# Reordering the side work of an attention and gated-unit kernel, and moving five kinds of loads

## The chip, the cores and the metric

The kernel runs on one core of a Trainium2 chip. The metric is the device time of one execution in microseconds; before the change it is 2025.47 us, the median of 3 runs (2024.54 to 2028.5). Times inside the kernel come from one profiled execution, which itself took 2024.75 us; its span from first to last instruction is 2022.6 us.

## The reference

Four batches of attention without a softmax, and then a gated linear unit over all 12032 rows. Shapes: u and v are 4 x 3008 x 256, z is 4 x 3008 x 64, w_gate and w_val are 256 x 1536 and w_out is 1536 x 256 (these three come in as 64-bit floats).

```python
scores = (1 / S) * z @ z.T            # per batch, S = 3008
attn = maximum(scores, 0) ** 2
x = u * (attn @ v)                    # 12032 rows of 256
gate = 1 / (1 + exp(-(x @ w_gate)))
out = (gate * (x @ w_val)) @ w_out
```

The scores of a batch are symmetric, so a block of them can be computed once and used turned for the mirrored block.

## The kernel before

**Two stages.** Attention fills the first 960 us of the span, the gated unit the rest. The change touches the first stage and the loads at its end. Every operand is split into a high and a low float32r part, so that three matmuls (or two, for the scores) make one product of full accuracy.

**Steps.** Attention is a list of 288 steps, 72 for each batch b: six chunks c of 512 queries (the last has 448), and for each chunk 12 pairs i of 128 keys, some computed and some mirrored from an earlier chunk. A step that is computed costs four score matmuls (L349, L350); ScalarE takes relu and square out of PSUM into the tile `r` (L357, L358) and rounds `r` to the high part `ah` (L373); VectorE subtracts to get the low part `al` (L378), and turns `r` for the mirrored blocks (L423, L427), which SP then stores to a DRAM tensor `shared` (L404, L409). A mirrored step loads its `r` back five steps ahead (L467) and goes straight to L373. Four steps of the first batch read blocks that were stored unturned (L464) and are turned late, on VectorE (L475). Then TensorE multiplies `ah` and `al` with the parts of v (L493, L495, L500). PSUM results of a chunk leave with one ScalarE copy (L515).

**Order within a step.** The order is written out by hand: the loop over g issues the scores of step g+2, the loads back of g+5, the stores of g, the turning of g+1, the late turning of g+2, then `run(before, g)`, then square, rounding and subtraction of step g+2, then `run(after, g)` and at last the matmuls of step g. Each engine works its own instructions in this order. `before` and `after` are tables of side work, filled ahead of the loop.

**Side work.** There are 18 jobs `Narrow`, which turn blocks of the 64-bit weights to float32 parts: each loads 512 KB of raw weights (L178), takes an absolute value on ScalarE one step later (L183), then bit operations on VectorE (L188 to L209), and stores the parts to DRAM (L233) for the second stage. Their first steps are 24 to 52, 84 to 126 and 156 to 198, seven steps apart; batch 3 (from step 216) has none. Other side work is the v of the next batch (load L293, high part L302, low part L308), its z (L258, L265, L268, L272), and at the end of attention the u rows (L551), their transposes (L559), the product x (L569), sums (L579) and parts (L583, L588) of the first group of the second stage, and the loads of its narrow weights (L603, L605).

All of these loads are issued by SP, one after the other. The raw areas are small rings: `raw_a` holds two v pairs and two pieces of z, `w_a` two raw weight blocks.

Of the kernel before, what the change touches and what calls it, by code (L numbers as in the profile page):

```python
# [26 lines left out]
def kernel(  # L27
# [16 lines left out]
    CH = 512  # L44
# [9 lines left out]
    def chunk(c):  # L54
        return min(CH, S - c * CH)
# [13 lines left out]
    v_a, z_a, zq_a, r_a, ah_a, al_a, al2_a, turned_a, raw_a, zt_a, keep_a, w_a, spare_a = map(area, sizes)  # L69
# [11 lines left out]
    def part(a, kb, cols, dt=F32):  # L81

        ap = a[:, int(kb * KB) : int(kb * KB) + cols]
        return ap if dt is F32 else ap.bitcast(dt)

    def f32(ap):
        return ap.bitcast(F32)
# [28 lines left out]
    def late(b, c):  # L116

        return (b, c) == (0, 0)

    def order(b, c):  # L120
        mirrored = [i for i in range(2 * c) if shared(b, i // 2, c)]
        own = [i for i in range(NPAIR) if i not in mirrored]
        last = []
        if halved(b, c):
            own.remove(2 * c + 1)
            last = [2 * c + 1]
        if not mirrored:
            return own + last
        own.sort(key=lambda i: (i // 2 > c, i // 2 < c and c < NCH - 1, i))
        m = len(own) + len(mirrored)  # L130
        places = [x * m // len(own) for x in range(len(own))]
        if (b, c) == (B - 1, NCH - 1):
            places = list(range(len(own)))
        line = [None] * m
        for x, i in zip(places, own):
            line[x] = i
        rest = iter(mirrored)
        return [next(rest) if i is None else i for i in line] + last

    steps = [(b, c, i) for b in range(B) for c in range(NCH) for i in order(b, c)]  # L140
    number = {s: g for g, s in enumerate(steps)}

    def back(s):
        return shared(s[0], s[2] // 2, s[1])
# [103 lines left out]
        return part(zq_a, 2 * ((b * NCH + p) % 2), CH, F32R)  # L248

    def load_z(b, p):  # L250
        t = part(w_a, 2 * p, CH) if b == 0 else part(raw_a, 4 + 2 * (p % 2), CH)
        t = t.rearrange("p (T d) -> p T d", d=32)
        n = chunk(p) // 32
        for g in range(4):
            d0 = 32 * (g % 2)
            src = z[b, p * CH : p * CH + 32 * n, d0 : d0 + 32].rearrange("(T p) d -> p T d", p=32)
            eng = nc.scalar if (b, p) == (0, 0) and g > 1 else nc.sync
            eng.dma_start(t[32 * g : 32 * g + 32, 0:n, :], src)  # L258
            if n < CH // 32:
                nc.sync.dma_start(t[32 * g : 32 * g + 32, n : n + 2, :], src[:, n - 2 : n, :])  # L260
        z_raw[b, p] = t.rearrange("p T d -> p (T d)")
# [8 lines left out]
    def z_low(b, p):  # L270
        hi, lo = z_place(b, p)
        nc.vector.tensor_tensor(lo, z_t[b, p], f32(hi), op=ALU.subtract)  # L272
# [13 lines left out]
        return (ap.rearrange("p (j d) -> p j d", j=2) for ap in (hi, lo))  # L286

    def load_v(b, i):
        t = part(turned_a, 2 * (i % 8), CH) if b == 0 else part(raw_a, 2 * (i % 2), CH)
        t = t.rearrange("p (j d) -> p j d", j=2)  # L290
        k0 = 256 * i
        if i < NPAIR - 1:
            nc.sync.dma_start(t, v[b, k0 : k0 + 256, :].rearrange("(p j) d -> p j d", j=2))  # L293
        else:
            nc.sync.dma_start(t[:, 0, :], v[b, k0 : k0 + P, :])
            for h in range(2):
                nc.sync.dma_start(t[64 * h : 64 * h + 64, 1, :], v[b, k0 + P : S, :])
        v_raw[b, i] = t
# [5 lines left out]
    def v_low(b, i):  # L304
        vh, vl = v_place(b, i)
        t = v_raw.pop((b, i))
        if i < NPAIR - 1:
            nc.vector.tensor_tensor(vl, t, f32(vh), op=ALU.subtract)  # L308
        else:
            nc.vector.tensor_tensor(vl[:, 0, :], t[:, 0, :], f32(vh[:, 0, :]), op=ALU.subtract)  # L310
            stacked = vh[64:128, 1, :]
            nc.vector.tensor_tensor(stacked, t[64:128, 1, :], f32(stacked), op=ALU.subtract)
# [6 lines left out]
    def r_of(s):  # L319
        return ring(r_a, 4, 5, s)  # L320

    def a_of(s):
        n = number[s] % 3
        al = part(al_a, 4 * n, 4 * KB, F32R) if n < 2 else part(al2_a, 0, 4 * KB, F32R)
        return ring(ah_a, 4, 3, s, F32R), al.rearrange("p (j q) -> p j q", j=2)
# [49 lines left out]
    def rest(s):  # L375
        n = chunk(s[1])
        r, (ah, al) = r_of(s), a_of(s)
        nc.vector.tensor_tensor(al[:, :, 0:n], r[:, :, 0:n], f32(ah[:, :, 0:n]), op=ALU.subtract)  # L378
# [74 lines left out]
    def as_stored(i):  # L453
        return part(keep_a, 4 * (i % 2), 2 * CH)
# [14 lines left out]
    def turn_late(s):  # L469
        b, c, i = s  # L470
        if back(s) and late(b, i // 2):
            src = as_stored(i).rearrange("p (B j a k) -> p k B j a", j=2, a=32, k=2)
            dst = r_of(s).rearrange("p k (B b j) -> p k B j b", b=32, j=2)
            for k in range(2):
                nc.vector.transpose(out=dst[:, k], in_=src[:, k])  # L475
# [230 lines left out]
    with tc.manual_schedule():  # L706
# [3 lines left out]
        before, after = {}, {}  # L710

        def at(when, g, f, *args):
            when.setdefault(g, []).append((f, args))

        def run(when, g):
            for f, args in when.get(g, ()):
                f(*args)

        per = NPAIR * NCH
        for b in range(1, B):  # L720
            g0 = (b - 1) * per
            for p in range(NCH):
                g = g0 + (3 * NPAIR + 4 * p if p < 3 else 4 * NPAIR + 4 * (p - 3) if p < 5 else 5 * NPAIR)
                if (b, p) == (1, 1):
                    g = 5 * NPAIR + 3
                at(after, g, load_z, b, p)
                at(before, g + 2, turn_z, b, p)
                at(before, g + 3, z_high, b, p)
                at(before, g + 3, z_low, b, p)
            line = [number[b - 1, NCH - 1, i] for i in range(NPAIR)]  # L730
            for i in range(1, NPAIR):
                line[i] = max(line[i], line[i - 1] + 1)
            for i in range(NPAIR):
                g = g0 + (2 * NPAIR + 4, 2 * NPAIR + 8, 3 * NPAIR + 2, 3 * NPAIR + 7)[i] if i < 4 else line[i - 4]
                at(after, g, load_v, b, i)
                at(before, g + 2, v_high, b, i)
                at(before, g + 2, v_low, b, i)
        for b in range(B):
# [3 lines left out]
        starts = [*range(24, 54, 7), *range(84, 127, 7), *range(156, 199, 7)][: 3 * NF]  # L742
        for n, g in enumerate(starts):
            job = Narrow(n)
            for x, name in enumerate(job.jobs):
                at(after if name in ("load", "store") else before, g + x, getattr(job, name))

        g = len(steps) - NPAIR  # L750
        for t in range(2):
            at(after, g, load_sums, 0, t)
        at(after, g, load_u, 0, 0)
        for i in (0, 1, 2):
            at(after, g, load_w, i)
        at(before, g + 2, turn_u, 0, 0)
        at(after, g + 2, load_u, 0, 1)
        at(before, g + 3, make_x, 0, 0)
        at(before, g + 4, turn_u, 0, 1)
        for i in (3, 4, 5, 7):  # L760
            at(after, g + 4, load_w, i)
        at(before, g + 5, make_x, 0, 1)
        for i in (T1, T3):
            at(before, g + 6, sum_x, 0, i)
# [56 lines left out]
        for g, (b, c, i) in enumerate(steps[:-2]):  # L821
            nxt = steps[g + 2]
            k = g % NPAIR
            early = g < NPAIR
            if g < 3:
                for _ in pe_pv(steps[g]):
                    pass
            pe_scores(nxt)
            if early:
                if k + 2 < NPAIR:  # L830
                    v_low(0, k + 2)
                if k + 5 < NPAIR:
                    load_v(0, k + 5)
                if k in (2, 3, 5):
                    z_low(0, {2: 3, 3: 4, 5: 5}[k])
                if k in (0, 2, 4):
                    turn_z(0, k // 2 + 3)
            if g + 5 < len(steps):
                load_back(steps[g + 5])
            if k == 1 and g > 1:  # L840
                keep(*steps[g - 2][:2], True)
            store_turned(steps[g])
            turn(steps[g + 1])
            turn_late(nxt)
            run(before, g)
            if not back(nxt):
                square(nxt)
            round_up(nxt)
            rest(nxt)
            if early and k + 3 < NPAIR:  # L850
                v_high(0, k + 3)
            if early and k in (1, 2, 4):
                z_high(0, {1: 3, 2: 4, 4: 5}[k])
            if k == 0 and g:
                keep(*steps[g - 1][:2], False)
            run(after, g)
            if g >= 3:
                for _ in pe_pv(steps[g]):
                    pass
# [51 lines left out]
        for J in range(last + 1):  # L911
# [29 lines left out]
            for c in (11, 22, 21, 12):  # L941
                f, t = c // 10 - 1, c % 10 - 1
# [47 lines left out]
```

## Time and profile before

| | |
|---|---|
| time, median of 3 runs | 2025.47 us |
| time of the profiled execution | 2024.75 us |
| span of the profiled execution | 2022.6 us |
| PE busy | 1951.4 us, 96% |
| DVE busy | 1381.6 us, 68% |
| ACT busy | 1115.9 us, 55% |
| mean granted TensorE clock | 0.987 |
| shares of the chain that ended last | PE 74%, DMA 7%, SPq 6%, ACT 5%, DVE 5%, issue 3% |

PE is TensorE, DVE VectorE, ACT ScalarE, POOL GpSimd; SPq is the queue in which SP issues transfers. The granted clock is a share of the full 2.4 GHz. The chain is followed back from the last instruction to whatever released each step.

### The profile page before, as it was taken

What the parts mean: (1) busy time and instruction counts of PE and PEld (TensorE: products, weight loads), DVE (VectorE), ACT (ScalarE), POOL (GpSimd) and SP (SyncE); (2) the same over time, 40 slices, a digit from 0 to 9 for tenths busy, and PEclk for the clock granted to TensorE, in tenths of its full rate; (3) what the DMA queues carried; (4) which work ended last, traced back from release to release, by engine and by line L of the source; (5) the groups of instructions that cost most, each with busy time, mean ns of one, the idle gap of its engine ahead of it and who ended that gap; (6) DMA issues with size and microseconds to landing.
All of it is one profiled execution on the core that took longest, in us unless ns stands there. A gap on an engine that the chain in (4) does not pass through costs nothing.

```text
span 2022.6 us, 25614 instructions
## 1 busy us (share of the span) xinstructions
PE 1951.4 (96%) x9086; PEld 1710.3 (85%) x9086; DVE 1381.6 (68%) x1702; ACT 1115.9 (55%) x1432; POOL 386.9 (19%) x325
## 2 busy tenths in 40 slices
PE   9987899999998999997999999999999999999998
PEld 7876788778887898886888888888888888888898
DVE  7676687776787777554666666767676676766664
ACT  7875687766886677764443443434344443434343
POOL 3000000000000000000333333333333333333333
PEclk9998999999999999998999999999999999999999
DMA  6676767897788967778611212121111212111110
GB/s 139 144 195 188 210 158 189 232 241 214 174 217 229 239 184 179 173 211 246 189 32 32 49 25 51 28 38 32 32 41 26 49 32 42 32 32 25 28 22 16
DMA packets 587984, 233.46 MB, mean 115 GB/s; under 512 B 528848, under 2 KB 546000, under 8 KB 587856
## 3 DMA queue, kind: packets, MB, share of 16 engines
q1 hardware_dynamic: 582576, 229.20, 45.8%
q0 software_dynamic: 1024, 2.10, 0.5%
q8 instruction: 71, 1.16, 0.2%
q10 hardware_dynamic: 4256, 0.52, 0.2%
q14 instruction: 57, 0.47, 0.1%
HBM read 127.01 MB, written 98.70 MB: 112 GB/s over the span
## 4 chain that ended last, share of the span: by engine, by line
PE 74%; DMA 7%; SPq 6%; ACT 5%; DVE 5%; issue 3%; DVEq 0%; ACTq 0%
PE banks L631 11%; PE banks L632 11%; PE banks L630 11%; PE banks L500 6%; PE banks L493 6%; PE banks L690 6%; PE banks L692 6%; PE banks L691 6%; PE banks L495 6%; ACT ah L373 2%; PE banks L350 2%; PE banks L349 2%; DVE al L378 2%; SPq L404 2%; DMA w<-in_moe_w_out_dram 2%
## 5 line engine op out<-in xcount | busy, mean ns | idle before, releaser
L674 POOL TENSOR_TENSOR h<-spare,h 128x512 fp32r<-128x512 f32 (+1 forms) x288 | 366.9, 1274 | 1597.0 <-ACT h L669 1596.6
L378 DVE TENSOR_TENSOR al<-r,ah 128x1024 fp32r<-128x1024 f32 (+1 forms) x287 | 342.5, 1196 | 223.8 <-ACT ah L373 217.7
L493 PE MATMUL banks<-ah,v 128*128 128x512 f32 (+1 forms) x1152 | 437.8, 383 | 45.5 <-ACT ah L373 44.5
L495 PE MATMUL banks<-ah,v 128*128 128x512 f32 (+1 forms) x1104 | 419.7, 380 | 0.0
L665 DVE TENSOR_TENSOR spare<-banks,spare 128x512 f32<-128x512 f32 (+1 forms) x288 | 195.6, 679 | 284.2 <-PE banks L632 280.6
L500 PE MATMUL banks<-al,v 128*128 128x512 f32 (+1 forms) x1152 | 347.8, 384 | 16.1 <-DVE al L378 13.7
L661 ACT ACTIVATE spare<-spare 128x512 f32<-128x512 f32 (+1 forms) x288 | 179.1, 622 | 275.3 <-DVE spare L655 268.0
L669 ACT ACTIVATE h<-spare 128x512 fp32r<-128x512 f32 (+1 forms) x288 | 178.6, 620 | 225.7 <-DVE spare L665 223.1
L493 PEld LDWEIGHTS banks<-ah,v 128*128 128x128 f32 x1152 | 222.1, 193 | 81.8 <-ACT ah L373 53.0
L373 ACT ACTIVATE ah<-r 128x1024 fp32r<-128x1024 f32 (+1 forms) x251 | 255.4, 1032 | 51.3 <-DMA r<-shared 19.9
L500 PEld LDWEIGHTS banks<-al,v 128*128 128x128 f32 x1152 | 218.4, 193 | 56.7 <-DVE al L378 30.7
L495 PEld LDWEIGHTS banks<-ah,v 128*128 128x128 f32 x1104 | 212.5, 192 | 25.3
L357 ACT ACTIVATE r<-banks 128x1024 f32<-128x1024 f32 (+2 forms) x173 | 167.0, 965 | 94.5 <-PE banks L350 91.8
L358 ACT ACTIVATE r<-r 128x1024 f32<-128x1024 f32 (+2 forms) x173 | 174.4, 1008 | 5.5
L630 PE MATMUL banks<-z,v 128*128 128x512 f32 x414 | 156.9, 379 | 0.0
L632 PE MATMUL banks<-z,v 128*128 128x512 f32 x414 | 156.9, 379 | 0.0
L631 PE MATMUL banks<-z,v 128*128 128x512 f32 x378 | 143.3, 379 | 0.0
L655 DVE TENSOR_TENSOR spare<-banks,spare 128x512 f32<-128x512 f32 (+1 forms) x144 | 117.9, 819 | 27.2 <-PE banks L632 24.2
L655 DVE TENSOR_TENSOR spare<-banks,zt 128x512 f32<-128x512 f32 (+1 forms) x144 | 116.4, 808 | 28.8 <-PE banks L632 28.7
L349 PE MATMUL banks<-zq,z 128*128 128x512 f32 (+2 forms) x348 | 126.7, 367 | 1.5 <-DVE zq L792 1.5
L350 PE MATMUL banks<-zq,z 128*128 128x512 f32 (+2 forms) x348 | 126.8, 367 | 0.0
L630 PE MATMUL banks<-v 128*128 128x512 f32 (+1 forms) x342 | 126.6, 370 | 0.0
(122 smaller groups left out, 3258.4 us busy)
## 6 DMA issues: line engine op xcount, KB each, us to landing
r<-shared SPq DMA_DIRECT2D x72, 512.0 KB, 4.3
shared<-turned SPq DMA_DIRECT2D x236, 128.0 KB, 2.7
r<-shared SPq DMA_DIRECT2D x38, 448.0 KB, 4.5
shared<-spare SPq DMA_DIRECT2D x128, 128.0 KB, 3.1
turned<-sums SPq DMA_DIRECT2D x22, 512.0 KB, 4.0
turned<-in_u_dram SPq DMA_DIRECT2D x176, 64.0 KB, 2.3
sums<-keep SPq DMA_DIRECT2D x20, 512.0 KB, 3.4
raw<-in_v_dram SPq DMA_DIRECT2D x33, 256.0 KB, 3.7
```

The lines of the kernel that those rows point to most:

```text
L373: nc.scalar.activation(ah[:, :, 0:n], r[:, :, 0:n], AF.Copy)
L378: nc.vector.tensor_tensor(al[:, :, 0:n], r[:, :, 0:n], f32(ah[:, :, 0:n]), op=ALU.subtract)
L493: nc.tensor.matmul(o, vh[:, j, ds], moving(ah[:, j, 0:n]), start=(k == 0 and j == 0), stop=False)
L495: nc.tensor.matmul(o, vl[:, j, ds], moving(ah[:, j, 0:n]), start=False, stop=False)
L500: nc.tensor.matmul(acc[:, d, 0:n], vh[:, j, ds], moving(al[:, j, 0:n]), start=False, stop=stop)
L630: nc.tensor.matmul(o, wt[:, 0, w], xh, start=(x == 0), stop=False)
L631: nc.tensor.matmul(o, wt[:, 0, w], xl, start=False, stop=False)
L632: nc.tensor.matmul(o, wt[:, 1, w], xh, start=False, stop=end)
L655: nc.vector.tensor_tensor(by_half(g_t[dst][:, 0:m]), product(bank(J, value, name)), product(other), op=ALU.add)
L661: nc.scalar.activation(g, g, AF.Sigmoid)
L665: nc.vector.tensor_tensor(g, product(bank(J, 1, c)), g, op=ALU.mult)
L674: nc.gpsimd.tensor_tensor(lo[:, 0:m], g_t[c][:, 0:m], f32(hi[:, 0:m]), op=ALU.subtract)
```

## The change

Five edits, all in the order and the placing of existing work; no instruction's size changes and no arithmetic is added.

1. In the loop, `run(before, g)` moves from ahead of the step's square, rounding and subtraction to behind them.
2. The late turning is issued for step g+3 in place of g+2, behind the step's own work.
3. A job's raw weights are loaded three steps earlier, so four steps ahead of their first use in place of one.
4. v is loaded one step earlier (three steps ahead in place of two); its ring in `raw_a` has three places in place of two, and z keeps one place in place of two.
5. Seven loads of narrow weights for the second stage move from steps 276 and 280 to steps 216, 220, ... 240.

```diff
@@ load_z
-        t = part(w_a, 2 * p, CH) if b == 0 else part(raw_a, 4 + 2 * (p % 2), CH)
+        t = part(w_a, 2 * p, CH) if b == 0 else part(raw_a, 6, CH)
@@ load_v
-        t = part(turned_a, 2 * (i % 8), CH) if b == 0 else part(raw_a, 2 * (i % 2), CH)
+        t = part(turned_a, 2 * (i % 8), CH) if b == 0 else part(raw_a, 2 * (i % 3), CH)
@@ tables
-                at(after, g, load_v, b, i)
+                at(after, g - 1, load_v, b, i)
...
-            for x, name in enumerate(job.jobs):
-                at(after if name in ("load", "store") else before, g + x, getattr(job, name))
+            at(after, g - 3, job.load)
+            for x, name in enumerate(job.jobs[1:], 1):
+                at(after if name == "store" else before, g + x, getattr(job, name))
...
-        for i in (0, 1, 2):
-            at(after, g, load_w, i)
+        for x, i in enumerate((0, 1, 2, 3, 4, 5, 7)):
+            at(after, 3 * per + 4 * x, load_w, i)
...
-        for i in (3, 4, 5, 7):
-            at(after, g + 4, load_w, i)
@@ loop over g
             turn(steps[g + 1])
-            turn_late(nxt)
-            run(before, g)
             if not back(nxt):
                 square(nxt)
             round_up(nxt)
             rest(nxt)
+            if g + 3 < len(steps):
+                turn_late(steps[g + 3])
+            run(before, g)
```

What this moves is seen at three places. First ScalarE, in chunk 3 of the first batch, around the fourth weight job: L183 is the absolute value that needs the loaded weights, L302 a high part of v, L227 the high part of the job ahead; the others are the steps' own. Before:

```order
L302 ACTIVATE v<-raw 128x512
L227 ACTIVATE w<-w 128x512
L357 ACTIVATE r<-banks 128x2x256
L358 ACTIVATE r<-r 128x2x256
L373 ACTIVATE ah<-r 128x1024
L183 ACTIVATE w<-w 128x512
L357 ACTIVATE r<-banks 128x1024
L358 ACTIVATE r<-r 128x1024
L373 ACTIVATE ah<-r 128x1024
L268 ACTIVATE z<-zt 128x512
```

and now:

```order
L302 ACTIVATE v<-raw 128x512
L227 ACTIVATE w<-w 128x512
L357 ACTIVATE r<-banks 128x1024
L358 ACTIVATE r<-r 128x1024
L373 ACTIVATE ah<-r 128x1024
L183 ACTIVATE w<-w 128x512
L373 ACTIVATE ah<-r 128x1024
L268 ACTIVATE z<-zt 128x512
```

The absolute value stands one step's work later: the square of 1024 columns that stood behind it now stands ahead of it.

Second SP, at the same job. L178 loads the raw weights, L404 and L409 store turned blocks, L464 and L467 load blocks back, L258 loads z, L293 v, L276 and L277 copy the queries, L233 stores the parts of the job ahead. Before:

```order
L276 DMA zq<-z 64x512
L277 DMA zq<-z 64x512
L293 DMA raw<-in_v_dram 128x512
L464 DMA keep<-shared_0_4_386 128x1024
L409 DMA shared_3_5_1229<-turned 32x16x32 x6
L258 DMA raw<-in_z_dram 32x16x32 x4
L464 DMA keep<-shared_0_4_386 128x1024
L178 DMA w<-in_moe_w_gate_dram 128x2x512
L233 DMA w_o<-w 128x512 x2
L467 DMA r<-shared_1_4_658 128x1024 x2
```

and now:

```order
L293 DMA raw<-in_v_dram 128x512
L276 DMA zq<-z 64x512
L277 DMA zq<-z 64x512
L178 DMA w<-in_moe_w_gate_dram 128x2x512
L464 DMA keep<-shared_0_4_386 128x1024
L409 DMA shared_3_5_1229<-turned 32x16x32 x6
L258 DMA raw<-in_z_dram 32x16x32 x4
L464 DMA keep<-shared_0_4_386 128x1024
L233 DMA w_o<-w 128x512 x2
L467 DMA r<-shared_1_4_658 128x1024 x2
```

The weight load has moved ahead of twelve transfers, two of them loads back (L464), and the v load ahead of the two query copies.

Third SP at the end of attention, from step 276: L540 and L551 load what the first group of the second stage needs, L603 and L605 its narrow weights. Before:

```order
L540 DMA turned<-sums 128x2x512 x2
L551 DMA turned<-in_u_dram 32x16x32 x8
L603 DMA wgv<-w_gv 128x1792
L605 DMA v<-w_gv 128x2x512
L603 DMA wgv<-w_gv 128x1792
L467 DMA r<-shared_2_5_5998 128x2x448
L513 DMA sums<-keep 256x1x512
L467 DMA r<-shared_2_5_5998 128x2x448
L551 DMA turned<-in_u_dram 32x16x32 x8
L467 DMA r<-shared_3_5_6225 128x2x448 x2
L605 DMA v<-w_gv 128x2x512
L603 DMA wgv<-w_gv 128x1792
```

and now:

```order
L540 DMA turned<-sums 128x2x512 x2
L551 DMA turned<-in_u_dram 32x16x32 x8
L467 DMA r<-shared_2_5_6006 128x2x448
L513 DMA sums<-keep 256x1x512
L467 DMA r<-shared_2_5_6006 128x2x448
L551 DMA turned<-in_u_dram 32x16x32 x8
L467 DMA r<-shared_3_5_6233 128x2x448 x2
L467 DMA r<-shared_4_5_6406 128x2x448 x2
```

The seven narrow-weight loads are gone from between the loads back; they now stand one by one among the stores of chunks 0, 1 and 2 of batch 3.

## Rows read from the trace of the kernel before

**Rows 1.** Waits of PE, first 960 us: total us, times, longest us.
```profile
PE banks L493 <- ACT ah L373: 44.5, 19, 8.6
PE banks L500 <- DVE al L378: 13.7, 10, 7.7
```

**Rows 2.** Waits of all engines over the span, same columns.
```profile
ACT v L302 <- DMA raw<-in_v_dram: 35.5, 25, 3.6
...
ACT w L183 <- DMA w<-in_moe_w_gate_dram: 27.5, 6, 8.4
ACT ah L373 <- DMA r<-shared: 19.9, 4, 10.0
ACT w L183 <- DMA w<-in_moe_w_val_dram: 18.1, 6, 6.3
...
ACT w L183 <- DMA w<-in_moe_w_out_dram: 16.7, 6, 4.3
...
ACT ah L373 <- DVE r L475: 12.4, 4, 3.6
```

**Rows 3.** Timelines (SP, ACT, PE), one weight job: start, us, instruction [idle before].
```profile
177.23 0.44 SPq L178 DMA_DIRECT2D w<-in_moe_w_gate_dram  x1
...
182.99 0.66 ACT L183 ACTIVATE w<-w 128x512 f32<-128x512 f32 x1 [8.38 <-DMA w<-in_moe_w_gate_dram]
...
185.68 1.06 ACT L373 ACTIVATE ah<-r 128x1024 fp32r<-128x1024 f32 x1
...
186.79 0.80 PE L493 MATMUL banks<-ah,v 128*128 128x512 f32 x1 [8.55 <-ACT ah L373]
```

**Rows 4.** L515 alone, from the view of one source line.
```profile
L515 ACT ACTIVATE keep<-banks x23: 899/1007/1018, 57.0 to 924.1; 128x1024 f32<-128x1024 f32 x20, 128x896 f32<-128x896 f32 x3
```

**Rows 5.** Windows, chunks 1-4: length, five engines' busy (x), PEclk, DMA, GB/s.
```profile
57.02:234.45 177.43, 154.12 (x678) 128.89 (x677) 123.11 (x137) 119.19 (x129) 0.00 (x0) 0.95 0.72 184
310.23:475.04 164.81, 151.04 (x662) 128.47 (x661) 122.43 (x142) 113.30 (x125) 0.00 (x0) 0.95 0.86 223
549.42:708.44 159.02, 148.18 (x662) 125.20 (x661) 119.56 (x136) 112.68 (x124) 0.00 (x0) 0.98 0.89 228
782.13:924.15 142.02, 142.02 (x669) 125.46 (x668) 85.60 (x72) 102.69 (x106) 0.00 (x0) 1.00 0.75 189
```

**Rows 6.** Timeline of PE: two neighbouring matmuls of 512 columns.
```profile
145.51 0.38 PE L495 MATMUL banks<-ah,v 128*128 128x512 f32 x1
145.73 0.38 PE L493 MATMUL banks<-ah,v 128*128 128x512 f32 x1
```

**Rows 7.** Windows: chunks 2-4 of batch 2, then three of 10 us.
```profile
589.98:708.44 118.46, 109.21 (x487) 92.54 (x486) 86.35 (x99) 81.58 (x92) 0.00 (x0) 0.97 0.91 237
...
640.00:650.00 10.00, 9.19 (x44) 7.75 (x43) 7.48 (x11) 5.76 (x7) 0.00 (x0) 1.00 1.02 245
650.00:660.00 10.00, 7.66 (x26) 5.52 (x25) 6.79 (x8) 6.81 (x8) 0.00 (x0) 0.83 1.00 296
...
980.00:990.00 10.00, 10.00 (x48) 8.77 (x47) 5.28 (x8) 3.79 (x6) 3.32 (x3) 1.00 1.01 410
```

**Rows 8.** Timelines of SP and of DVE at the end of attention.
```profile
923.08 6.73 SPq L551 DMA_DIRECT2D turned<-in_u_dram  x8
929.86 0.49 SPq L603 DMA_DIRECT2D wgv<-w_gv  x1
...
931.66 0.53 SPq L467 DMA_DIRECT2D r<-shared  x1
...
933.64 11.70 SPq L551 DMA_DIRECT2D turned<-in_u_dram  x8
...
947.59 1.25 DVE L559 STREAM_TRANSPOSE turned<-turned 128x1024 f32<-128x1024 f32 x1 [11.26 <-DMA turned<-in_u_dram]
...
962.07 1.22 DVE L588 TENSOR_TENSOR zq<-turned,z 128x1024 fp32r<-128x1024 f32 x1
```

**Rows 9.** The loads back, L467, from issue to landing.
```profile
DMA to landing us min/median/max: 3.4/4.5/11.0
```

## The prediction

> **What bounds the kernel now.** I read the engines' busy shares first: PE leads with 96% of the span, so time can come back only where PE stands still or is fed late. Next the waits of PE alone: in the first 960 us it waits 44.5 us in 19 places for the high part `ah` from ScalarE and 13.7 us in 10 places for the low part `al` from VectorE [rows 1]. Only the attention stage has such waits, and the change touches only that stage.
>
> Third, the waits of the engines that feed PE. ScalarE waits 27.5 + 18.1 + 16.7 = 62.3 us, 18 times, at L183 for the raw weights; 35.5 us, 25 times, at L302 for raw v; 12.4 us, four times, at L373 for late turning; and 19.9 us, four times, for loads back [rows 2]. How such a wait reaches PE is read from one weight job [rows 3]: SP issues the load at 177.23, ScalarE sits at L183 for 8.38 us until 182.99, the step's own rounding L373 stands behind it and starts at 185.68, and PE, which waits for that, has been idle 8.55 us when it starts at 186.79.
>
> Last, what all of it costs, half-speed matmuls behind the waits included. L515 copies each chunk out, so its rows mark the chunks [rows 4]. Between the marks chunks 1 to 4 of the four batches took 177.43, 164.81, 159.02 and 142.02 us [rows 5]. Batch 3 has no weight job and no v or z to fetch; its window has PE busy for all 142.02 us at a granted clock of 1.00, against 0.95, 0.95 and 0.98 in the others. Batches 1 and 2 do the same matmuls, so their excess is 22.8 and 17.0 us. Batch 0 computes four more score pairs in these chunks (blocks that it cannot mirror), 16 matmuls at 0.22 us [rows 6], 3.5 us; its excess is 177.43 - 142.02 - 3.5 = 31.9 us. Together 71.7 us can come back there. The first and last chunk of a batch I leave as they are, the end of attention apart.
>
> **The change, part by part.** *Weights three steps earlier, and side work behind the step's own.* A step of batch 3 takes 142.02 / 48 = 2.96 us, so three steps are 8.9 us. The load of rows 3 was used 5.8 us after its issue, and the longest wait of the 18 is 8.4 us [rows 2]: nearly all go to nothing, by the move alone. The reordering is a second cover: L183 stands behind the step's L373, so the step that is due does not wait even where the load is late. It costs nothing by itself: the same instructions run, and in batch 1 VectorE is busy for 122.43 and ScalarE for 113.30 of 164.81 us [rows 5]. Where the cover goes, a side job of about a microsecond delays the next square.
>
> *v one step earlier, late turning one step sooner.* One more step is 2.96 us against a longest wait for v of 3.6, on average 1.4; the late turning's 3.1 us on average [rows 2] also fit in one step. These waits lie in the same chunks and are in the 71.7 us; a gain beyond that I exclude, since batch 3 shows PE without a gap. The smaller z ring holds a piece for two steps and the next comes four later: no wait. SP now waits at some v loads for VectorE's L308, which stands behind L378; behind SP queue loads back, with five steps of lead. Between nothing and one SP hold of the length of L378, I take nothing.
>
> *What the transfers allow.* The loads keep their bytes, and the stretch is to shrink. Share times length gives the DMA time that each stretch needs: 0.72 x 177.43 = 127.7, 0.86 x 164.81 = 141.7, 0.89 x 159.02 = 141.5 us [rows 5], beside 145.5, 142.0 and 142.0 us of matmuls. Batches 1 and 2 would need the DMA engines full without a pause. Over 118 us they held 0.91, with the stalls in it, and over 20 us 1.01 [rows 7]. I take 0.95, between the two: batch 1 takes 149.2 us and gives back 15.6, batch 2 148.9 and 10.1; batch 0 needs 134.4, stays bound by matmuls and gives back all 31.9. With 0.91 the three give 31.9 + 9.1 + 3.5 = 44.5, with 1.01 all 71.7.
>
> Here a rule speaks against me. The share of DMA time in these rows is 0.86 and 0.89 at 223 and 228 GB/s. The Trainium skill (Perfetto Trace Analysis, Identifying the Most-Contended Engine) says to judge DMA by HBM utilization and not by occupancy, which misleads with 16 engines. This case's trace agrees in part: a window at 1.01 moved 410 GB/s and one at 1.02 only 245 [rows 7]. By the rule the transfers would not bound and the sum would hold 71.7 us; by the rows it holds 57.6.
>
> *The narrow weights.* At the end SP issues eight u loads in 6.73 us, then three narrow-weight loads from 929.86 until 931.66, then the next load back; the second eight u loads, behind these transfers, take 11.70 us in place of 6.73 [rows 8]. Without the weights the second eight end 1.8 + 5.0 = 6.8 us sooner, and with them the turning at 947.59 that waited 11.26 us for u. From there to the last part at 962.07 it is 14.5 us of VectorE, which stays, so PE's first group begins some 6.6 us sooner (0.2 off for the VectorE work that fills the gap), though all four waits for loads back, 19.9 us, lie there. Where the seven loads go, to steps 216 to 240, the trace shows nothing: PE has no gap and the DMA share is 0.75 [rows 5]. Below, nothing; below nothing is excluded, as no wait is there to remove. Above, seven times the mean wait for a load back, 19.9 / 4 = 5.0 us, 35 us. With a quarter of the DMA time free I take one such wait, 5.0 us.
>
> *Sum.* 31.9 + 15.6 + 10.1 + 6.6 - 5.0 = 59.2 us. The profiled execution took 2024.75 us, 0.7 below the median of 2025.47; so 1965.6 against its own time and 1966 against the median.
>
> **Rivals.** *The queue takes the place of the weights.* Each raw load now stands ahead of loads back that ScalarE needs. Those land in 4.5 us at the median and 11.0 at most [rows 9], against a lead of about three steps, 8.9 us. If every second raw load makes one late by the mean of 5.0 us, 45 us come back as waits for `r`, and 5.0 for the narrow weights: 71.7 + 6.6 - 50 = 28 us of gain, 1997. For it: DMA near full. Against it: in batches 0 to 2 no wait of that name is long enough to appear; the 19.9 us lie at the end of attention, behind narrow-weight loads [rows 8].
>
> *Slower.* The same mechanism at all 18 raw loads: 18 x 5.0 = 90 us against 78.3 us removed, 2025.5 + 11.7 = 2037. It decides from 78.3 / 18 = 4.4 us of lateness per load. A load back would have to land in 8.9 + 4.4 = 13.3 us, past the longest seen.
>
> *All of it comes back.* Transfers close up when the engines stop waiting, as the window with 410 GB/s shows they can with longer rows [rows 7], and the narrow weights cost nothing: 71.7 + 6.6 = 78.3, 1947. This is what the Trainium skill's rule on HBM utilization (Perfetto Trace Analysis, same section) would make of it. Against it: the short rows of the turned blocks, at 1.02 and 245 GB/s, are these very stretches.
>
> *It doesn't do what it says.* SP itself is late, so that the loads, though earlier in its order, start no earlier: the eight u loads show SP held 11.70 us over work of 6.73 [rows 8]. The waits stay, 2025. Against it: the load of rows 3 passes twelve transfers in SP's order; at the 6.73 / 8 = 0.84 us of the first u loads that is 10 us of issuing.
>
> **How the numbers follow.** Forecast 0.62, queue 0.14, all back 0.14, slower 0.05, no effect 0.05. The forecast's own range is 1946 (1.01, no cost) to 1990 (0.91 and most of the 35 us). The range for 8 in 10, 1944 to 1999, takes in the case of all back and the upper half of the queue's; slower and no effect lie outside. A measurement of this kernel tells 0.2%, 4 us, from no change. Faster: 0.62 + 0.14 + 0.14, 0.90. Within 0.2%: 0.04. Slower: 0.06, the slower case and a fifth of no effect.
>
> **What would show it.** Right: the waits at L183 and L302 fall from 97.8 us to under 15; PE's waits in the first 960 us from 58 to some 20, mostly at the end of attention; chunks 1 to 4 of batches 1 and 2 near 149 us with a DMA share of 0.95; the clock at 1.00 there; PE's first matmul of the second stage some 54 to 60 us sooner. Wrong: a wait of ScalarE for `r` loaded back in batches 0 to 2 (the queue); a share above 0.97 or stretches at 142 us (all back); L183 still waiting (no effect). A gap in steps 216 to 240 would show the narrow weights dearer than 5 us. The second stage should keep its length; if it does not, I have missed a link.

## The result and the profile after

The changed kernel takes 1964.56 us, the median of 4 runs (1962.23 to 1966.38), against 2025.01 us for the kernel before; the ratio is 0.970, with a 95% interval of 0.968 to 0.972. The profiled execution has a span of 1962.6 us, 60.0 less than before, and a mean granted clock of 0.998 in place of 0.987.

The waits of PE over the whole span of the kernel after (total us, times, longest), beside [rows 1]:

```profile
PE banks L500 <- DVE al L378: 9.1, 11, 3.8
PE banks L349 <- DMA zq<-z: 7.7, 4, 2.7
PE banks L493 <- ACT ah L373: 3.9, 3, 1.8
```

44.5 us of waits for `ah` have become 3.9, and 13.7 for `al` have become 9.1. The second line is new: PE waits four times for the copy of a chunk's queries.

The waits of ScalarE in the same view, beside [rows 2]:

```profile
ACT z L268 <- DVE zt L265: 27.6, 19, 3.7
ACT ah L373 <- DMA r<-shared: 22.8, 14, 4.7
...
ACT ah L373 <- DVE r L475: 10.1, 4, 3.5
...
ACT v L302 <- DMA raw<-in_v_dram: 3.8, 3, 1.8
```

No wait of L183 for a load is left (62.3 us before), and the waits for v fell from 35.5 us to 3.8. The late turning is the one that hardly moved, 12.4 to 10.1. Of the 14 waits for loads back, 11 (12.0 us) lie in batches 1 and 2 and three at the end of attention; before, all four lay at the end.

Chunks 1 to 4 of the four batches, between the L515 copies as in [rows 5] (length; busy time of PE, weight loads, VectorE, ScalarE, GpSimd; granted clock, DMA share, GB/s):

```profile
56.87:209.73 152.86, 147.42 (x678) 125.90 (x677) 122.89 (x137) 119.96 (x129) 0.00 (x0) 1.00 0.84 216
284.76:432.22 147.46, 142.36 (x662) 123.52 (x661) 121.80 (x141) 115.03 (x125) 0.00 (x0) 1.00 0.94 245
507.31:655.18 147.87, 143.77 (x662) 124.77 (x661) 119.40 (x136) 114.10 (x125) 0.00 (x0) 0.99 0.92 242
730.44:872.46 142.02, 142.02 (x669) 125.46 (x668) 85.62 (x72) 102.68 (x105) 0.00 (x0) 1.00 0.80 206
```

They gave back 24.6, 17.4 and 11.2 us, 53.1 together; batch 3 is the same to the hundredth, at a DMA share of 0.80 in place of 0.75. The DMA share of batches 1 and 2 rose from 0.86 and 0.89 to 0.94 and 0.92.

The timeline of SP at the end of attention of the kernel after (start, us, instruction), beside [rows 8]:

```profile
871.40 6.58 SPq L551 DMA_DIRECT2D turned<-in_u_dram  x8
878.08 0.52 SPq L467 DMA_DIRECT2D r<-shared  x1
...
881.35 5.68 SPq L551 DMA_DIRECT2D turned<-in_u_dram  x8
887.13 2.49 SPq L467 DMA_DIRECT2D r<-shared  x4
```

and of VectorE there:

```profile
889.18 1.25 DVE L559 STREAM_TRANSPOSE turned<-turned 128x1024 f32<-128x1024 f32 x1 [4.39 <-DMA turned<-in_u_dram]
...
902.40 1.22 DVE L588 TENSOR_TENSOR zq<-turned,z 128x1024 fp32r<-128x1024 f32 x1
```

The second eight u loads take 5.68 us in place of 11.70. From the last L515 copy into `keep`, which ends chunk 4 of batch 3 (924.15 before, 872.46 after), to the last part L588 it is 29.9 us in place of 37.9: 8.0 us. The first chunks of the batches kept their 40.6 us; the last chunks lost 1.5 us in sum (35.17, 33.76, 33.07 before; 34.41, 34.47, 34.63 now). 53.1 + 8.0 - 1.5 = 59.6 of the 60.0 by which the span fell; from the last L588 on both kernels take 1060 us.

### The profile page after: what moved, and what is told of

It reads as the page before. It is cut to its first block, busy times and chain, and to the rows that moved or that the text cites. A ratio compares the mean times of both kernels' runs of the same rounds, so it can differ in the third digit from the quotient of the medians.

```text
span 1962.6 us, 25589 instructions
## 1 busy us (share of the span) xinstructions
PE 1930.3 (98%) x9086; PEld 1702.9 (87%) x9086; DVE 1380.3 (70%) x1702; ACT 1119.3 (57%) x1432; POOL 387.2 (20%) x325
## 3 DMA queue, kind: packets, MB, share of 16 engines
q0 software_dynamic: 1024, 2.10, 0.5%
## 4 chain that ended last, share of the span: by engine, by line
PE 87%; SPq 3%; DVE 3%; ACT 2%; DMA 2%; issue 1%; DVEq 0%; ACTq 0%
PE banks L631 12%; PE banks L632 12%; PE banks L630 12%; PE banks L500 10%; PE banks L493 9%; PE banks L495 9%; PE banks L690 6%; PE banks L692 6%; PE banks L691 6%; PE banks L349 3%; PE banks L350 3%; DVE al L378 1%; SPq L258 1%; ACT ah L373 1%; SPq L409 1%
## 5 line engine op out<-in xcount | busy, mean ns | idle before, releaser
L378 DVE TENSOR_TENSOR al<-r,ah 128x1024 fp32r<-128x1024 f32 (+1 forms) x287 | 341.4, 1192 | 193.5 <-ACT ah L373 188.6
L493 PE MATMUL banks<-ah,v 128*128 128x512 f32 (+1 forms) x1152 | 429.9, 377 | 4.3 <-ACT ah L373 3.9
L495 PE MATMUL banks<-ah,v 128*128 128x512 f32 (+1 forms) x1104 | 414.8, 376 | 0.0
L500 PE MATMUL banks<-al,v 128*128 128x512 f32 (+1 forms) x1152 | 340.7, 377 | 9.9 <-DVE al L378 9.1
L493 PEld LDWEIGHTS banks<-ah,v 128*128 128x128 f32 x1152 | 218.5, 190 | 32.4 <-ACT ah L373 5.9
L495 PEld LDWEIGHTS banks<-ah,v 128*128 128x128 f32 x1104 | 209.6, 190 | 24.6
L655 DVE TENSOR_TENSOR spare<-banks,spare 128x512 f32<-128x512 f32 (+1 forms) x144 | 117.8, 818 | 27.5 <-PE banks L632 24.6
```

The source lines that it names most:

```text
L493: nc.tensor.matmul(o, vh[:, j, ds], moving(ah[:, j, 0:n]), start=(k == 0 and j == 0), stop=False)
L495: nc.tensor.matmul(o, vl[:, j, ds], moving(ah[:, j, 0:n]), start=False, stop=False)
L500: nc.tensor.matmul(acc[:, d, 0:n], vh[:, j, ds], moving(al[:, j, 0:n]), start=False, stop=stop)
L655: nc.vector.tensor_tensor(by_half(g_t[dst][:, 0:m]), product(bank(J, value, name)), product(other), op=ALU.add)
```

## The experiments

Theory: ScalarE and VectorE work in order, so a side job that waits for a load holds the step that stands behind it; loading earlier and standing behind the step's own work are two covers against the same wait. The DMA engines, nearly full, bound what comes back in batches 1 and 2. Rivals: only one of the two covers does the work; or what is left comes from the order of SP's queue. Times are medians of 4 runs (5 for both queue edits), ratios are against the kernel before on the same chip; "chunks" is the length of chunks 1 to 4 of all batches in the profile (643.3 us before, 590.2 after).

| run | time, us | ratio (95%) | chunks, us |
|---|---|---|---|
| early raw loads alone | 1986.65 | 0.980 (0.979 to 0.982) | 605.9 |
| reordering alone | 2001.09 | 0.987 (0.985 to 0.989) | 615.9 |
| after, edit 1 undone | 1970.01 | 0.972 (0.971 to 0.974) | 598.1 |
| after, edit 2 undone | 1971.88 | 0.973 (0.971 to 0.975) | 597.9 |
| after, edit 3 undone | 1994.27 | 0.984 (0.982 to 0.986) | 619.7 |
| after, edit 4 undone | 1964.09 | 0.969 (0.967 to 0.970) | 591.1 |
| after, edit 5 undone | 1974.74 | 0.975 (0.973 to 0.976) | 591.0 |
| after, query copies sooner | 1961.43 | 0.968 (0.966 to 0.969) | 590.3 |
| after, half of the raw loads | 1960.58 | 0.968 (0.966 to 0.969) | 587.1 |
| after, side transfers on GpSimd's queue | 1960.46 | 0.968 (0.966 to 0.970) | 587.3 |
| both queue edits | 1961.39 | 0.968 (0.966 to 0.970) | 586.3 |
| both, and the end block sooner | 1956.41 | 0.965 (0.963 to 0.967) | 588.6 |

**One cover at a time.** The kernel before with the early raw loads alone:

```diff
-            for x, name in enumerate(job.jobs):
-                at(after if name in ("load", "store") else before, g + x, getattr(job, name))
+            at(after, g - 3, job.load)
+            for x, name in enumerate(job.jobs[1:], 1):
+                at(after if name == "store" else before, g + x, getattr(job, name))
```

> The kernel before with edit 3 alone (raw weights three steps earlier); side work still stands ahead of the step's own. Theory (ScalarE is held by loads that have not landed; either cover removes that): the 62 us of waits at L183 go to under 5, the 35 us at L302 stay, chunks 1 to 4 of batches 0 to 2 give back some 40 of the 53 us that the whole change gave, 1980 to 1990. Rival (what counts is the place of side work in the step, since any job ahead of the square delays it): L183 stops waiting but at most 20 us come back, 2005 or more.

L183 waited for no load, and the chunks gave back 37.4 us. Two lines of the waits of all its engines (total us, times, longest):

```profile
ACT v L302 <- DMA raw<-in_v_dram: 53.1, 26, 6.3
...
PE banks L493 <- ACT ah L373: 18.0, 10, 3.7
```

The waits for v grew from 35.5 to 53.1 us, where the theory had them stay. The v loads themselves landed as fast as before (3.7 us at the median, against 3.8), so presumably ScalarE, no longer held at the weights, reaches the v jobs earlier. The theory's time came.

The kernel before with the reordering alone:

```diff
-            run(before, g)
             if not back(nxt):
                 square(nxt)
             round_up(nxt)
             rest(nxt)
+            run(before, g)
```

> The kernel before with edit 1 alone (side work behind the step's own; loads as before). Theory: the second cover works by itself: L183 still waits, some 20 to 40 us in all, but behind the step's rounding, so PE's waits in chunks 1 to 4 halve: 25 to 40 us come back, 1985 to 2000. Rival of the early load (order alone is nothing, a load that is late holds ScalarE wherever it stands): under 10 us, 2015 or more.

The time fell by 26 us though L183 still waited 44.4 us for loads, as its waits show:

```profile
ACT w L183 <- DMA w<-in_moe_w_gate_dram: 19.6, 4, 6.8
...
ACT w L183 <- DMA w<-in_moe_w_val_dram: 13.1, 3, 5.5
ACT w L183 <- DMA w<-in_moe_w_out_dram: 11.7, 5, 4.6
```

The rival that order is nothing is out. The waits for v fell to 15.7 us by the order alone. L183 and L302 together wait 60.1 us in place of 97.8, and the chunks are 27.4 us shorter: that a wait costs PE less behind the step's rounding than ahead of it does not follow from this run, since the waits themselves became shorter.

**Each cover undone.** The kernel after with the raw loads one step ahead again (the diff of the first run backwards):

> The kernel after without edit 3: raw weights loaded one step ahead again. Theory (the reordering is a second cover, smaller than the first): L183 waits 20 to 40 us again, behind the rounding; a third of that reaches PE: 1970 to 1985. Rival (the reordering alone is enough): within 3 us of after.

1994.27 us, 30 us slower than after, and worse than either expectation. L183 waited 53.2 us for loads in 12 places, 4.4 us on average and up to 7.1 where a step takes 2.96; the waits of this kernel:

```profile
ACT w L183 <- DMA w<-in_moe_w_gate_dram: 21.7, 4, 7.1
ACT w L183 <- DMA w<-in_moe_w_out_dram: 16.9, 5, 5.8
ACT w L183 <- DMA w<-in_moe_w_val_dram: 14.6, 3, 6.1
```

All of these waits lie behind the step's rounding, and they made the chunks 29.5 us longer. So for the weights that place is a cover in part only: the three longest waits at L183, 7.1, 6.5 and 6.1 us, were followed by waits of PE for `ah` of 3.4, 4.3 and 4.5, where 8.4 us at L183 in the job of [rows 3], ahead of the rounding, went with 8.6 of PE. The rounding of the next step stands behind the wait.

The kernel after with the side work ahead of the square again:

```diff
             turn(steps[g + 1])
+            run(before, g)
...
                 turn_late(steps[g + 3])
-            run(before, g)
```

> The kernel after without edit 1: side work ahead of the step's square again, the other four edits kept. Theory (the early loads are the first cover, the reordering a second one that is worth what ScalarE and VectorE lose to landed side work): chunks 1 to 4 of batches 0 to 2 some 6 to 12 us longer in all than after, L183 without a wait for DMA: 1970 to 1977. Rival (with the loads early the order does not matter): within 3 us of after.

1970.01 us, 5 us slower. ScalarE waits for v again, 27.1 us where the kernel after has 3.8, and PE's largest waits are those for `al`, 20.2 us where the kernel after has 9.1; VectorE's side work now stands ahead of L378:

```profile
ACT v L302 <- DMA raw<-in_v_dram: 27.1, 13, 5.5
PE banks L500 <- DVE al L378: 20.2, 14, 4.8
```

So the early load is worth 30 us on top of the rest, the reordering 5, and alone 40 and 26: they cover the same wait, and the early load covers more of it.

**v, late turning, narrow weights.** The kernel after with v and z as before:

```diff
-        ... part(raw_a, 6, CH)
+        ... part(raw_a, 4 + 2 * (p % 2), CH)
-        ... part(raw_a, 2 * (i % 3), CH)
+        ... part(raw_a, 2 * (i % 2), CH)
-                at(after, g - 1, load_v, b, i)
+                at(after, g, load_v, b, i)
```

> The kernel after without edit 4: v loaded two steps ahead into a ring of two, z with two places. Theory (the v loads now stand ahead of the query copies and make PE wait 7.7 us for these): those waits go, L302 waits 10 to 25 us again but behind the step's own work, and the time is 2 to 8 us lower than after, 1957 to 1963. Rival (v early is worth its cost): waits for v reach PE and the time is 5 to 15 us higher, 1970 to 1980.

Neither came: 1964.09 us, as after. PE's waits for the query copies fell to 2.8 us and L302 waited 24.9 us again:

```profile
ACT v L302 <- DMA raw<-in_v_dram: 24.9, 17, 4.2
...
PE banks L349 <- DMA zq<-z: 2.8, 3, 1.3
```

PE's waits for `ah` and `al` are 16.4 us in place of 13.0, so the two nearly made up for each other. Edit 4 is worth nothing here. These waits for v, 1.5 us on average and shorter than a step, stand behind the step's own work and cost next to nothing: here the second cover holds, better than for the longer waits at L183.

The kernel after with the late turning back at step g+2:

```diff
             turn(steps[g + 1])
+            turn_late(nxt)
...
-            if g + 3 < len(steps):
-                turn_late(steps[g + 3])
```

> The kernel after without edit 2: late turning for step g+2 and ahead of the step's square again. Theory (four instances in batch 0 alone; ScalarE waited for them 12.4 us before and 10.1 after, so the edit moved little): within 2 us of after, batch 0's chunks 1 to 4 within 2 us of 152.9. Rival (one step sooner is what batch 0 needed): batch 0 longer by 3 us or more.

The theory missed and the rival came: 1971.88 us. Its waits have ScalarE waiting 18.3 us for the late turning, not 10.1:

```profile
ACT ah L373 <- DVE r L475: 18.3, 4, 6.5
```

and its window of chunks 1 to 4 of batch 0 is 7.1 us longer than that of the kernel after:

```profile
57.02:216.94 159.92, 149.24 (x678) 126.86 (x677) 122.74 (x137) 119.80 (x130) 0.00 (x0) 0.99 0.80 205
```

Four turnings of some 1.4 us are worth 7 us of batch 0. Why each costs more than its own length is read from the timelines of ScalarE and VectorE at the first of them. With edit 2 undone VectorE works side jobs (L308, L195) and a turning (L423) ahead of it:

```profile
130.29 1.23 DVE L378 TENSOR_TENSOR al<-r,ah 128x1024 fp32r<-128x1024 f32 x1 [1.06 <-ACT ah L373]
131.44 0.69 DVE L308 TENSOR_TENSOR v<-raw,v 128x512 fp32r<-128x512 f32 x1
132.04 0.82 DVE L195 SCALAR_TENSOR_TENSOR w<-w 128x512 int32<-128x512 int32 x1
132.78 0.85 DVE L423 STREAM_TRANSPOSE spare<-r 128x512 f32<-128x512 f32 x1
133.49 1.61 DVE L475 STREAM_TRANSPOSE r<-keep 128x512 f32<-128x512 f32 x2
135.20 1.06 ACT L373 ACTIVATE ah<-r 128x1024 fp32r<-128x1024 f32 x1 [4.42 <-DVE r L475]
```

In the kernel after it stands right behind the subtraction of the step ahead:

```profile
129.00 1.06 ACT L373 ACTIVATE ah<-r 128x1024 fp32r<-128x1024 f32 x1
130.09 1.23 DVE L378 TENSOR_TENSOR al<-r,ah 128x1024 fp32r<-128x1024 f32 x1 [1.07 <-ACT ah L373]
131.23 1.60 DVE L475 STREAM_TRANSPOSE r<-keep 128x512 f32<-128x512 f32 x2
132.93 1.06 ACT L373 ACTIVATE ah<-r 128x1024 fp32r<-128x1024 f32 x1 [2.36 <-DVE r L475]
```

The other three of the run have side work or a turning ahead of them too; the longest, 6.5 us, stands behind a side job that itself waited 3.5 us for z. The second piece shows also why ScalarE still waits in the kernel after: rounding, subtraction and turning follow one another, and from one rounding to the next it is 3.9 us, more than a step.

The kernel after with the narrow weights at steps 276 and 280 again:

```diff
-        for x, i in enumerate((0, 1, 2, 3, 4, 5, 7)):
-            at(after, 3 * per + 4 * x, load_w, i)
+        for i in (0, 1, 2):
+            at(after, g, load_w, i)
...
+        for i in (3, 4, 5, 7):
+            at(after, g + 4, load_w, i)
```

> The kernel after without edit 5: the seven narrow-weight loads stay at steps 276 and 280. Theory (they delay the u loads and the loads back at the end): chunks 0 to 5 of all batches as after, and the way from the last L515 copy to the last part L588 is 6 to 10 us longer: 1971 to 1975. Rival (the end became shorter because the loads back had less to wait for elsewhere): within 2 us of after.

As the theory had it: 1974.74 us, the chunks as after (591.0), and the second u loads slow again, as the timeline of SP shows,

```profile
883.06 11.28 SPq L551 DMA_DIRECT2D turned<-in_u_dram  x8
```

with the last part on VectorE at

```profile
911.80 1.22 DVE L588 TENSOR_TENSOR zq<-turned,z 128x1024 fp32r<-128x1024 f32 x1
```

From the last L515 copy at 872.49 it is 39.3 us, 9.4 more than after.

**What is left.** One of the new waits, in the timeline of SP of the kernel after:

```profile
382.74 0.98 SPq L293 DMA_DIRECT2D raw<-in_v_dram  x1
383.81 0.49 SPq L276 DMA_DIRECT2D zq<-z  x1
384.34 0.59 SPq L277 DMA_DIRECT2D zq<-z  x1
```

and in that of PE, with its idle time at the end of the row:

```profile
387.72 0.46 PE L349 MATMUL banks<-zq,z 128*128 128x512 f32 x1 [2.15 <-DMA zq<-z]
```

The v load that edit 4 put ahead of the query copies (the second order piece above) is issued in front of them; with edit 4 undone 2.8 of the 7.7 us are left, so some 5 are owed to it. The kernel after with the copies sooner:

```diff
-                    at(after, b * per + NPAIR * p - 6, z_both, b, p)
+                    at(after, b * per + NPAIR * p - 9, z_both, b, p)
```

> The kernel after with the copies of the queries (L276, L277) three steps earlier. Theory (they land late behind a v load and stores, and PE waits 7.7 us in four places): PE's waits for zq go to zero and 5 to 8 us come back, 1957 to 1960. Rival (the transfers are the bound there, so PE waits for something else in their place): waits for al and ah grow by as much, within 2 us of after.

The waits for the copies went, and PE's other waits between 280 and 690 us grew from 1.8 and 2.2 us in the kernel after to these:

```profile
PE banks L493 <- ACT ah L373: 4.9, 4, 1.8
PE banks L500 <- DVE al L378: 4.2, 4, 1.3
```

So of 7.7 us, 5.1 turned into other waits. The time is 3 us lower, and the two intervals overlap. In the profile the gain lies in the last chunks of batches 1 and 2, 32.9 us each in place of 34.5 and 34.6; chunks 1 to 4 kept their sum. Next, half of each raw load left out:

```diff
-                self.t.rearrange("p (k f) e -> p k (f e)", k=2), src.rearrange("(k p) f -> p k f", p=P)
+                self.t.rearrange("p (k f) e -> p k (f e)", k=2)[:, 0:1], src.rearrange("(k p) f -> p k f", p=P)[:, 0:1]
```

> The kernel after with half of each raw weight load left out (256 KB in place of 512; half of the weights are then not the reference's). Theory (the DMA engines, at a share of 0.92 to 0.94 in chunks 1 to 4 of batches 1 and 2, bound what is left): these chunks come down by 2 to 5 us each towards 142.02, PE's waits fall by a third, 1952 to 1960. Rival (what is left comes from the order of SP's queue, not from the bytes): within 2 us of after.

Its windows of chunks 1 to 4 of batches 1 and 2, columns as above:

```profile
283.05:430.67 147.62, 143.72 (x662) 124.77 (x661) 121.37 (x141) 115.09 (x125) 0.00 (x0) 0.99 0.92 235
505.11:651.37 146.26, 142.10 (x662) 123.61 (x661) 119.49 (x136) 114.14 (x125) 0.00 (x0) 1.00 0.91 234
```

Batch 1 did not move (147.46 to 147.62), batch 2 gave 1.6 us, with six loads (1.5 MB) less than before in the one and five (1.3 MB) in the other (the last of the 18 jobs begins at step 191, not 198). How much a stretch scatters by itself shows the kernel with edit 2 undone, an edit that touches batch 0 alone; its windows of batches 1 and 2:

```profile
291.96:440.73 148.77, 142.78 (x664) 123.87 (x663) 122.21 (x141) 115.00 (x126) 0.00 (x0) 1.00 0.93 242
515.67:662.84 147.17, 142.19 (x662) 123.53 (x661) 119.58 (x136) 113.90 (x125) 0.00 (x0) 1.00 0.93 243
```

They differ by +1.3 and -0.7 us from the kernel after. So the two stretches did not come down by the 2 to 5 us of the theory, which speaks against bytes as their bound. It does not settle it: the time, 1960.58 us, is 4.0 lower than after and lies between the two expectations, with 1.6 us from batch 0 and 2.0 from the last chunks of batches 1 and 2. Then the same bytes on another queue:

```diff
-            nc.sync.dma_start(            # raw weights, weight parts, v of batches 1 to 3
+            nc.gpsimd.dma_start(
```

> The kernel after with the raw weight loads, the stores of the weight parts and the v loads of batches 1 to 3 issued by GpSimd's queue in place of SP's; the same bytes. Theory (DMA engines bound what is left): within 3 us of after. Rival (SP's one queue, in order, bounds it: loads back and query copies stand behind side transfers): the waits for zq and al go, 8 to 15 us come back, 1950 to 1957.

The same two windows:

```profile
285.71:431.26 145.55, 142.39 (x663) 123.62 (x662) 122.17 (x141) 114.79 (x125) 14.01 (x24) 1.00 0.94 251
504.60:650.34 145.74, 142.31 (x662) 123.53 (x661) 119.67 (x136) 114.05 (x125) 13.26 (x23) 1.00 0.94 247
```

Batches 1 and 2 gave 1.9 and 2.1 us, little more than the scatter, but in both; their last chunks are at 32.7 and 32.9, and batch 0 gave nothing (153.96). PE's waits for the query copies fell from 7.7 to 0.8 us; those for `al`, which the rival had going too, are 10.4. The time, 1960.46 us, lies between the two expectations and is the same as with half of the raw loads, so by the time alone bytes and queue are not told apart. The two queue edits together:

> The kernel after with both: side transfers (raw weights, weight parts, v) on GpSimd's queue and the query copies three steps earlier. Theory (both cure the same waits for zq, so they do not add up; what is left in batches 1 and 2 is DMA-bound at 0.94): 1957 to 1961, chunks 1 to 4 of these batches near 145.5 us as with GpSimd's queue alone. Rival (they add up): 1953 to 1956.

1961.39 us, no better than one of them: they cure the same waits, those for the query copies, of which none is left here. And with the block at the end three steps sooner:

```diff
-        g = len(steps) - NPAIR
+        g = len(steps) - NPAIR - 3
```

> The same as e9_pool_zq with the whole block at the end of attention (loads of sums and u, transposes, x, sums, parts) begun three steps, some 8 us, earlier. Theory (the second stage's start is bound by the u loads and the VectorE chain behind them): PE's waits behind the last L515 copy, 5.2 us with the change, fall under 1.5 and 4 to 6 us come back against e9_pool_zq: 1952 to 1956, the best of all. Rival (the earlier u loads delay the loads back by as much): within 2 us of e9_pool_zq.

1956.41 us, the lowest of all; its interval (0.963 to 0.967) lies just below that of the kernel after (0.968 to 0.972) and overlaps that of the run with both queue edits alone (0.966 to 0.970). The last part L588 starts 20.9 us behind the last copy at 867.68, in place of 29.9, in the timeline of VectorE:

```profile
888.61 1.22 DVE L588 TENSOR_TENSOR zq<-turned,z 128x1024 fp32r<-128x1024 f32 x1
```

so all parts are there before PE's first matmul of the second stage, which in the kernel after came 3.1 us ahead of the last part:

```profile
892.77 0.38 PE L630 MATMUL banks<-z,wgv 128*128 128x512 f32 x1
```

PE still waits 3.2 us for `al` behind the last copy, more than the 1.5 that I expected. From the last copy to the end of the span it is 3.9 us less than with both queue edits alone (1086.3 against 1090.2), but chunks 1 to 4 are 2.3 us longer, and the two profiled spans differ by 1.1 us only.

## Why the prediction was right

The time was 1964.56 us where 1966 was forecast, in the main by the mechanism that was named: ScalarE no longer waits for the weights, and PE no longer for ScalarE. That the sum came within 1.4 us is luck in part, since the gain of batch 0 was put 7.3 us too high and the 5.0 us of cost for the narrow weights did not come. The terms, point by point:

- *Weights and order.* Right for the early load: L183 and L302 were to fall from 97.8 us to under 15, and they are at 3.8. The two single runs and the two undone ones show that either edit works alone and that the early load is worth more. The reason given for the second cover, that the due step does not wait even where the load is late, holds for the short waits for v and only in part for the weights: with edit 3 undone 53.2 us of waits behind the rounding cost 30 us.
- *Batch 0, 31.9 us.* Too high; it gave 24.6. One step that failed is that late turning fits in one step and its waits go: they stayed at 10.1 us, and PE's waits in these chunks at 5.1. Even the forecast's own 3.1 us is more than a step of 2.96, and the turning stands behind a rounding and a subtraction, 3.9 us in all. The run with edit 2 undone shows how much hangs on it. Whether this is the whole of the 7.3 us that are missing is not shown.
- *Batches 1 and 2, 15.6 and 10.1 us.* They gave 17.4 and 11.2, at DMA shares of 0.94 and 0.92 where 0.95 was taken. The size is right; the reason is not shown. The DMA time that was held fixed at 141.7 and 141.5 us, share times length, came out as 0.94 x 147.46 = 138.6 and 0.92 x 147.87 = 136.0 for nearly the same bytes. With half of the raw bytes gone the lengths stayed within their scatter, and with the side transfers on another queue they shrank by some 2 us at a share of 0.94. So it is not shown that this share is the limit. The waits for the query copies are owed to SP's queue, since they go when the side transfers leave it; whether by its order or by the time that SP takes to issue is not separated. What holds the stretches above 142.02 us (5.4 and 5.9 us in the kernel after, 3.5 and 3.7 with GpSimd's queue) stays open.
- *All back* priced these chunks at 71.7 us. They gave 53.1. The Trainium skill (Perfetto Trace Analysis, Identifying the Most-Contended Engine) says to judge DMA by HBM utilization, because occupancy misleads with 16 engines. The half-load run agrees with the warning, as far as the scatter lets it: shares of 0.92 and 0.91, and lengths that moved by +0.2 and -1.6 us. The time that this rival drew from the rule did not come.
- *The end, 6.6 us.* It gave 8.0, and its undoing cost 9.4. The last chunks, which were left as they are, lost 1.5 us.
- *Narrow weights, 5.0 us of cost.* Nothing: batch 3 has 142.02 us as before. This error of 5.0 us and the one of 7.3 in batch 0 nearly cancel, which is luck. (The upper end of the forecast's own range, 1990, takes 15.6 of the 35 us and not most of them; with all 35 it would be 2009.)
- *v, nothing for SP's hold.* No cost of the hold is seen (edit 4 undone takes as long), but the v loads stand ahead of the query copies, which I had in the order and did not price: some 5 of the 7.7 us of PE's waits for these. The 20 us of PE's waits that were forecast came, but only 3.8 of them lie at the end of attention, where most were expected.
- *The queue takes the place.* In small: the waits for loads back that were named as a sign of being wrong are there now in batches 1 and 2, 12.0 us in 11 places, but little of it reaches PE, which waits 1.8 us for `ah` there.

## What to carry to other kernels

A job that waits for a load and stands in an in-order engine's stream ahead of the work that the critical engine needs can cost that engine its whole wait, as in the job of [rows 3]; here, taking 62.3 us of such waits away gave 37.4. Load it earlier first, then put it behind the due work; that place covers a wait that is shorter than a step, and only a part of a longer one. Price an excess by a stretch of the same kernel that does the same matmuls without the disturbance: it holds the waits, the low clock and the ragged restarts in one number. And when loads are moved forward, list what they now stand in front of, the small late copies above all.

## What was not expected of the hardware

At DMA shares of 0.94 and 0.92, taking 256 KB out of each of 18 loads moved two stretches of 147 us by +0.2 and -1.6 us, while issuing the same bytes from GpSimd's queue moved them by -1.9 and -2.1 at shares of 0.94. Such a stretch scatters by about 1 us by itself. A share near one did not mean that 4% fewer bytes would shorten the stretch by as much.
